# Decode attention with a gated MLP on one core: two heads per cache tile, and the values as the moving operand of the product with the probabilities

## The chip, the cores and the metric

The kernel runs on one core of one Trainium2 chip. The metric is device time in microseconds (us). The numbers below are medians. The profile is of one execution; its span is 1.7 to 1.9 us shorter than the time of the same execution. In the views, PE stands for the matmuls of TensorE, PEld for its weight loads, DVE for VectorE, ACT for ScalarE, POOL for GpSimd and SP for SyncE. A packet is one piece that a DMA engine moves at a time, for K and V one row of one partition (in the kernel before 16 KB, 613 ns in the median).

## The reference

This is one decode step: four sequences, one new token each, 32 heads with 8192 cached keys and values of 128 elements, then a gated MLP. Everything in memory is bf16.

```python
B, D = 4, 512;  H, Sk, Dh = 32, 8192, 128;  F = 1792

def attn(x, k_cache, v_cache, wq, wo):             # caches: B x H x Sk x Dh
    q = (x @ wq).reshape(B, 1, H, Dh).transpose(0, 2, 1, 3)
    scores = einsum("bhqd,bhkd->bhqk", q, k_cache) * Dh ** -0.5
    p = softmax(scores)
    o = einsum("bhqk,bhkd->bhqd", p, v_cache)
    return o.transpose(0, 2, 1, 3).reshape(B, 1, H * Dh) @ wo

def mlp(x, w_gate, w_up, w_down):
    return (sigmoid(x @ w_gate) * (x @ w_up)) @ w_down

h  = x + attn(layernorm(x), k_cache, v_cache, wq, wo)
h2 = h + mlp(layernorm(h), w_gate, w_up, w_down)
```

There are 128 pairs of sequence and head. Each has 2 MB of keys (K) and 2 MB of values (V), so the caches are 537 MB of the 550.8 MB that must be read. Each byte is used once.

## The kernel before

The kernel has its own small scheduler. Each operation `P(engine, function, deps)` is put on one engine's list in program order, and its dependencies become semaphore waits. The parts that the change touches are these.

Loads go through one queue, issued in order by SyncE, into a ring of 8 slots of 2 MB. One load fills a slot with one head: 128 partitions, each a row of 16 KB. A load waits until the operation that consumed its slot's last content has ended. The loads of the output weights (`wo`) go into the buffer `kT`, so they wait for the last score.

```python
NS = 8                                             # slots
items = [("wq", 0)]
for t in range(NT + LAG):                          # NT = 128 heads, LAG = 10
    if t < NT:    items.append(("k", t))
    if t >= LAG:  items.append(("v", t - LAG))
    if NT + 1 <= t <= NT + NWO:  items.append(("wo", t - NT - 1))   # 8 loads of 512 KB
items += [("wg", 0), ("wu", 0), ("wd", 0)]         # wd in two pieces

def kv_src(t, cache):
    return cache[t // H, t % H, :, :].rearrange("(p r) d -> p (r d)", p=128)
...
for it in items:
    for op in dma_of[it]:
        op.deps = [sc_of[NT - 1]] if it[0] == "wo" else [consumed[p] for p in prev_of[it]]
```

VectorE transposes each K tile into `kT` (line 366, four operations of 128x1024 uint32 per head, 1213 ns each). TensorE then computes scores with q as weights (line 383, 16 matmuls of 512 columns per head). Eight heads share one softmax chain. The product with V uses each 128x128 block of V as *weights* and one column of probabilities as the moving operand, 64 times per head:

```python
# pe_pv, line 406
for r in range(r0, r1):                            # 64 blocks of V
    c0 = (r % 16) * 32 + (r // 16) * 8 + hh
    mm = e.matmul(ob[:, hh:hh + 1], ringv(slot)[:, r * 128:(r + 1) * 128],
                  PT_sb[:, g % 2, c0:c0 + 1], start=(r == 0), stop=(r == R - 1))
```

At the end, the down projection has the hidden vector as weights and `w_down` moving; the residual had been put into the accumulator by four small matmuls beforehand.

```python
for i, (t0, t1) in enumerate(WD_PARTS):            # [(0, 10), (10, 14)]
    for s_ in range(2):
        ...                                        # line 602
        for t in range(t0, t1):
            mm = e.matmul(bP[s_][0:B, 0:HD], hh_sb[:, B * t:B * t + B],
                          wd_v[:, t, HD * s_:HD * s_ + HD], ...)     # 256 columns
```

## Time and profile before

| | before |
|---|---|
| time, median of the first 3 runs (lowest to highest) | 1318.3 us (1317.25 to 1318.69) |
| span of the profile | 1316.8 us |
| bytes from HBM | 550.77 MB |
| packets for K and V | 32,640 of 16 KB, median 613 ns; 256 of 8 KB |
| packets on the instruction queue | 92 |

The first view is the profile's page: the span, the busy times of the engines, the DMA totals, two of its queues (packets, MB, share of 16 engines), and three of its costliest groups (line, engine, operation, shapes, count, then busy us and mean ns of one, then idle time before it and what ended it).

```profile
span 1316.8 us, 24848 instructions
PE 527.4 (40%) x11822; PEld 330.1 (25%) x11822; DVE 628.7 (48%) x639; ACT 39.2 (3%) x87; POOL 9.7 (1%) x17
DMA packets 44757, 552.37 MB, mean 419 GB/s; under 512 B 4328, under 2 KB 10224, under 8 KB 11248
q1 hardware_dynamic: 44648, 550.79, 98.9%
q8 instruction: 92, 1.51, 0.5%
...
L366 DVE STREAM_TRANSPOSE kT<-ring 128x1024 uint32<-128x1024 uint32 x512 | 592.3, 1213 | 596.6 <-DMA ring<-in_A_k_cache_dram 596.6
L406 PEld LDWEIGHTS PS<-PT_sb,ring 128*128 128x128 bf16 x8192 | 230.1, 104 | 114.6 <-issue 76.6
L406 PE MATMUL PS<-PT_sb,ring 128*128 128x1 bf16 x8192 | 239.2, 165 | 38.0 <-DMA ring<-in_A_v_cache_dram 35.3
```

No engine is busy half of the time, while the queue of loads is busy 98.9% of it.

A table of stretches of the span: stretch and length, then for each engine its busy time and count, then the TensorE clock that the throttle granted (1.00 is full speed), the mean DMA share of 16 engines, and the rate.

```profile
core 0: us, PE busy (x) PEld busy (x) DVE busy (x) ACT busy (x) POOL busy (x), PEclk, DMA share, GB/s
400.00:1200.00 800.00, 318.06 (x7170) 197.92 (x7170) 383.52 (x384) 15.46 (x40) 0.00 (x0) 0.50 1.01 427
...
1218.00:1236.00 18.00, 5.98 (x113) 3.13 (x114) 9.58 (x9) 0.00 (x0) 0.00 (x0) 0.50 0.74 314
1236.00:1251.00 15.00, 7.86 (x282) 7.33 (x279) 1.33 (x6) 3.03 (x6) 0.00 (x0) 0.50 0.99 395
```

For 800 us the stream runs without a gap. Near the end, from 1218 to 1236 us, the mean share drops to 0.74. The waits of the queue itself (us in total, times, longest) give the reason: the first of the `wo` loads waits at the head of the queue for the last score.

```profile
SPq L207 <- PE PS L383: 27.6, 1, 27.6
```

The last view is the end of the chain of waits (start, length, what):

```profile
1286.08 22.63 DMA ring<-in_B_w_down_dram
1308.70 0.14 issue
1308.84 5.76 PE PS L602 x28
1314.60 0.02 issue
1314.62 0.41 DVE o_sb L607
```

### The profile page before, as it was taken

What the parts mean: (1) busy time and instruction counts of PE and PEld (TensorE: products, weight loads), DVE (VectorE), ACT (ScalarE), POOL (GpSimd) and SP (SyncE); (2) the same over time, 40 slices, a digit from 0 to 9 for tenths busy, and PEclk for the clock granted to TensorE, in tenths of its full rate; (3) what the DMA queues carried; (4) which work ended last, traced back from release to release, by engine and by line L of the source; (5) the groups of instructions that cost most, each with busy time, mean ns of one, the idle gap of its engine ahead of it and who ended that gap; (6) DMA issues with size and microseconds to landing.
All of it is one profiled execution on the core that took longest, in us unless ns stands there. A gap on an engine that the chain in (4) does not pass through costs nothing.

```text
span 1316.8 us, 24848 instructions
## 1 busy us (share of the span) xinstructions
PE 527.4 (40%) x11822; PEld 330.1 (25%) x11822; DVE 628.7 (48%) x639; ACT 39.2 (3%) x87; POOL 9.7 (1%) x17
## 2 busy tenths in 40 slices
PE   2453433433343343443343343343334334344435
PEld 1122222222232232222222222222222223222334
DVE  6965445445444544544545444544544544554300
ACT  3000000000000000000000000000000000000000
POOL 2000000000000000000000000000000000000000
PEclk8555555555555555555555555555555555555555
DMA  9999999999999999999999999999999999999896
GB/s 397 425 428 427 427 429 425 427 426 427 426 428 427 426 427 427 426 428 428 425 429 427 427 427 427 426 428 427 426 427 427 427 427 426 428 426 428 351 408 258
DMA packets 44757, 552.37 MB, mean 419 GB/s; under 512 B 4328, under 2 KB 10224, under 8 KB 11248
## 3 DMA queue, kind: packets, MB, share of 16 engines
q1 hardware_dynamic: 44648, 550.79, 98.9%
q8 instruction: 92, 1.51, 0.5%
q14 instruction: 9, 0.07, 0.0%
q10 hardware_dynamic: 8, 0.00, 0.0%
HBM read 550.77 MB, written 0.00 MB: 418 GB/s over the span
## 4 chain that ended last, share of the span: by engine, by line
DMA 85%; DVE 12%; issue 2%; PE 1%; SPq 0%
DMA ring<-in_A_k_cache_dram 77%; DVE kT L366 11%; DMA ring<-in_A_v_cache_dram 6%; DMA ring<-in_B_w_down_dram 2%; DMA ring<-in_A_wq_dram 1%; PE PS L602 0%; DVE Lq L349 0%; PE PS L406 0%; PE PS L307 0%; DVE ring L324 0%; PE PS L383 0%; PE PS L334 0%; SPq L241 0%; SPq L207 0%; DVE o_sb L607 0%
## 5 line engine op out<-in xcount | busy, mean ns | idle before, releaser
L366 DVE STREAM_TRANSPOSE kT<-ring 128x1024 uint32<-128x1024 uint32 x512 | 592.3, 1213 | 596.6 <-DMA ring<-in_A_k_cache_dram 596.6
L383 PE MATMUL PS<-kT,Lq 128*32 128x512 bf16 x2048 | 242.9, 623 | 664.3 <-DVE kT L366 664.3
L406 PEld LDWEIGHTS PS<-PT_sb,ring 128*128 128x128 bf16 x8192 | 230.1, 104 | 114.6 <-issue 76.6
L406 PE MATMUL PS<-PT_sb,ring 128*128 128x1 bf16 x8192 | 239.2, 165 | 38.0 <-DMA ring<-in_A_v_cache_dram 35.3
L383 PEld LDWEIGHTS PS<-kT,Lq 128*32 128x32 bf16 x2048 | 57.3, 126 | 751.4 <-DVE kT L366 680.5
L445 ACT ACTIVATE negm<-PS 128x1 f32<-128x1 f32 x16 | 2.7, 171 | 1166.9 <-PE PS L441 1166.9
L456 PE MATMUL PS<-LS,onesf 128*128 128x8 f32 x32 | 9.5, 372 | 64.9 <-DVE LS L452 64.9
L478 DVE TENSOR_TENSOR OT<-PS,rinv 128x8 bf16<-128x8 f32 (+2 forms) x17 | 2.0, 115 | 52.0 <-PE PS L406 52.0
L456 PEld LDWEIGHTS PS<-LS,onesf 128*128 128x128 f32 x32 | 8.0, 312 | 66.6 <-DVE LS L452 66.5
L467 PE MATMUL PS<-Sel,E_sb 128*32 128x32 bf16 x1024 | 11.4, 192 | 2.8 <-issue 1.7
L424 DVE TENSOR_REDUCE mx<-PS 128x1 f32<-128x512 f32 x16 | 10.5, 657 | 2.0 <-PE PS L383 2.0
L441 PEld LDWEIGHTS PS<-onesf,rowx 1*128 1x128 f32 x32 | 8.0, 307 | 12.6 <-issue 12.6
L447 ACT ACTIVATE E_sb<-PS,negm 128x512 bf16<-128x512 f32 x16 | 11.0, 687 | 0.5
L473 ACT ACTIVATE PT_sb<-PS 128x512 bf16<-128x512 f32 x16 | 9.6, 597 | 27.5 <-PE PS L467 27.5
L467 PEld LDWEIGHTS PS<-Sel,E_sb 128*32 128x32 bf16 x1024 | 9.5, 103 | 3.2 <-issue 1.8
L441 PE MATMUL PS<-onesf,rowx 1*128 1x1 f32 x32 | 9.3, 358 | 0.0
L259 POOL MEMSET Lq<- 128x8208 f32 x1 | 6.9, 6937 | 0.0
L349 DVE CAST Lq<-PS 32x128 bf16<-32x128 f32 x8 | 5.7, 712 | 2.1 <-PE PS L334 1.9
L602 PE MATMUL PS<-ring,hh_sb 128*4 128x256 bf16 x28 | 5.7, 397 | 1.8 <-DMA ring<-in_B_w_down_dram 1.8
L277 DVE TENSOR_SCALAR xpad<-x_bf,lnst 4x512 bf16<-4x512 bf16 x1 | 6.0, 5981 | 0.0
L430 PE MATMUL PS<-identf,mx 128*1 128x128 f32 x16 | 5.9, 371 | 0.0
L348 ACT ACTIVATE Lq<-PS 32x128 bf16<-32x128 f32 x8 | 5.7, 715 | 4.2 <-PE PS L334 4.0
(69 smaller groups left out, 71.3 us busy)
## 6 DMA issues: line engine op xcount, KB each, us to landing
ring<-in_A_k_cache_dram SPq DMA_DIRECT2D x128, 2048.0 KB, 34.6
ring<-in_A_v_cache_dram SPq DMA_DIRECT2D x127, 2048.0 KB, 35.8
ring<-in_A_wq_dram SPq DMA_DIRECT2D x1, 4096.0 KB, 12.5
kT<-in_A_wo_dram SPq DMA_DIRECT2D x8, 512.0 KB, 17.1
ring<-in_A_v_cache_dram SPq DMA_DIRECT2D x2, 1024.0 KB, 20.7
ring<-in_B_w_gate_dram SPq DMA_DIRECT2D x1, 1792.0 KB, 20.9
ring<-in_B_w_up_dram SPq DMA_DIRECT2D x1, 1792.0 KB, 25.3
ring<-in_B_w_down_dram SPq DMA_DIRECT2D x1, 1280.0 KB, 22.6
```

The lines of the kernel that those rows point to most:

```text
L259: zlq = pool(lambda e: e.memset(Lq[:, :].bitcast(FP32), 0.0))
L277: d_x = P("dve", lambda e: e.tensor_scalar(xpad[0:B, :], x_bf[0:B, :], st[0:B, 0:1], st[0:B, 4:5], op0=ALU.subtract, op1=ALU.mult), [d_r, zx])
L366: return e.transpose(kT[:, buf, i * q:(i + 1) * q].bitcast(U32), ringv(src)[:, i * q:(i + 1) * q].bitcast(U32))
L383: mm = e.matmul(bS[g % 2][32 * j:32 * (j + 1), :], Lq[:, l0:l0 + 32], rhs, start=(hh == 0 and v == 0), stop=(hh == GH - 1 and v == 3), til ...
L406: mm = e.matmul(ob[:, hh:hh + 1], ringv(slot)[:, r * 128:(r + 1) * 128], PT_sb[:, g % 2, c0:c0 + 1], start=(r == 0), stop=(r == R - 1))
L424: mx_of[g] = P("dve", lambda e: e.tensor_reduce(mx[:, :], bS[g % 2][:, :], AX.X, ALU.max), [sc_of[g * GH + GH - 1], p1_of.get(g - 1)])
L430: p1_of[g] = P("pe", lambda e: e.transpose(bX[0:1, 0:128], mx[:, :], identf[:, :]), [mx_of[g], c_identf, d3_of.get(g - 1)] + ([o for ops i ...
L441: p2_of[g] = P("pe", lambda e: e.matmul(bX[:, 0:1], rowx[0:1, :], onesf[0:1, 0:1], start=True, stop=True), [d2b_of[g], c_ones])
L447: exp_of[g] = P("act", lambda e: e.activation(E_sb[:, :], bS[g % 2][:, :], ACT.Exp, bias=negm[:, 0:1], scale=SCALE, accum_out=sig[:, 0:1]) ...
L456: L_of[g] = P("pe", lambda e: e.matmul(bX[:, 0:GH], onesf[:, :], LS[:, :], start=True, stop=True), [LS_of[g], a1_of[g], c_ones])
L467: mm = e.matmul(bP[g % 2][32 * a:32 * (a + 1), 32 * rr:32 * rr + 32], E_sb[:, 32 * rr:32 * rr + 32], Sel[:, a, :], start=True, stop=True, ...
L473: ptc_of[g] = P("act", lambda e: e.activation(PT_sb[:, g % 2, :], bP[g % 2][:, :], ACT.Copy), [pt_of[g]] + last_pv)
```

## The change

Its intent is to read the caches in rows twice as long, and to replace the weight loads of the product with V by long moving operands. It has these parts.

- A tile holds two heads, 64 partitions each, with rows of 32 KB. The ring has 4 slots of 4 MB: the same bytes.
- The weights of the product with V are now columns of probabilities, padded with zeros to 32 columns so that each head and half of a tile adds into its own rows of the accumulator. V moves, 512 columns at a time: 16 matmuls per step in place of 64.
- The accumulator then holds more than is wanted; for every 8 heads it is scaled by the reciprocal sums, the wanted diagonal is gathered by four fp32 matmuls with a selection matrix, and copied to `OT`.
- The `wo` loads are queued among the last V loads. The last V tile comes in three pieces.
- `w_down` comes in three pieces and becomes the weights. An addition of the residual, one transposing matmul and a copy follow.

The diff, cut to its core:

```diff
-NS = 8
+NS = 4
@@ order of loads
-            if NT + 1 <= t <= NT + NWO:
-                items.append(("wo", t - NT - 1))
+            for i in {LAG2 - 4: (0, 1), LAG2 - 3: (2, 3, 4), LAG2 - 2: (5, 6, 7)}.get(t - NT2, ()):
+                items.append(("wo", i))
@@ source of a K or V tile
-            return cache[t // H, t % H, :, :].rearrange("(p r) d -> p (r d)", p=128)
+            h = 2 * t
+            return cache[h // H, h % H:h % H + 2, :, :].rearrange("h (p r) d -> (h p) (r d)", p=64)
@@ product with V
-                for r in range(r0, r1):
-                    c0 = (r % 16) * 32 + (r // 16) * 8 + hh
-                    mm = e.matmul(ob[:, hh:hh + 1], ringv(slot)[:, r * 128:(r + 1) * 128],
-                                  PT_sb[:, g % 2, c0:c0 + 1], start=(r == 0), stop=(r == R - 1))
+                for j in range(j0, j1):
+                    for rq in range(4):
+                        r0 = (u * 4 + j) * 16 + 4 * rq
+                        l0 = PZ0 + (rq * 32 + 8 * j + 4 * u + i) * 32 - 8 * i
+                        mm = e.matmul(bO[g % 2][32 * rq:32 * (rq + 1), :], PTz[:, g % 2, l0:l0 + 32],
+                                      ringv(slot)[:, r0 * 128:(r0 + 4) * 128],
+                                      start=(s % GS == 0 and j == 0), stop=(s % GS == GS - 1 and j == 3),
+                                      tile_position=(0, 32 * rq))
@@ after each group of 8
+        def chain_z(g):
+            z_of[g] = P("dve", lambda e: e.tensor_scalar(Zs[:, :], bO[g % 2][:, :], rinv[:, g % 2:g % 2 + 1], None,
+                                                         op0=ALU.mult), ...)
+        def chain_ot(g):
+                for r in range(4):
+                    mm = e.matmul(bX[:, 256:264], Zs[:, 128 * r:128 * (r + 1)], SelZ[:, r, :], start=(r == 0), stop=(r == 3))
+        def chain_otc(g):
+            otc_of[g] = P("dve", lambda e: e.tensor_copy(OT[:, 8 * g:8 * g + 8], bX[:, 256:264]), [ot_of[g]])
@@ down projection
-                        mm = e.matmul(bP[s_][0:B, 0:HD], hh_sb[:, B * t:B * t + B], wd_v[:, t, HD * s_:HD * s_ + HD],
-                                      start=False, stop=(t == NFT - 1), skip_group_check=True)
+                    for c in range(NDC):
+                        mm = e.matmul(bH[:, B * c:B * c + B], wd_v[:, t, 128 * c:128 * (c + 1)],
+                                      hh_sb[:, B * t:B * t + B], ...)
+        d_o = P("dve", ... h2 + bH -> oT ...)
+        p_o = P("pe", lambda e: e.matmul(bP[0][0:NB, 0:128], oT[:, :], ident[:, :], start=True, stop=True), ...)
+        o0 = P("dve", lambda e: e.tensor_copy(o_sb[:, :], bP[0][0:NB, 0:128]), [p_o])
```

Cut: setting up the selection matrices, the re-indexing of scores and softmax for two heads, `wq` read in rows of 32 KB, the weights of gate and up in one slot, and the writing of the padded probabilities.

## The prediction

> **What bounds it now.** The HBM read stream. The table of stretches shows 427 GB/s and a DMA share of 1.01 in every stretch from 40 to 1200 us; the page has VectorE busy 48%, TensorE 40%. The chain of waits is 85% DMA; its transposes of K only mark slots coming free. Mid-run work on TensorE (PV busy 239 us) and VectorE is off the critical path. Three other costs:
>
> 1. A hole near the end. The output-weight loads wait in the SP queue for the last score (27.6 us in its own waits); from 1218 to 1236 us the share is 0.74 (314 GB/s). The DMA records sum the idle to 5.0 us.
> 2. The tail after the last w_down piece (landed 1308.8): 28 matmuls of 256 columns, 5.74 us, a 0.4 us copy, the store.
> 3. A fixed cost in each packet. Median packet times: 1 KB 46 ns, 3.5 KB 140, 8 KB 309, 16 KB 613: slope about 27.2 B/ns (16 engines: 435 GB/s), intercept about 8.4 ns.[...]
>
> **What the change does.**
> - K and V: 32768 packets of 16 KB become 16384 of 32 KB. Estimate from the fit: 1216 ns each against 2 x 613 = 1226; 8 packets per engine and load, 128 loads: about 0.08 x 128 = 8 to 10 us with the halved completion packets. I take 8.
> - The hole: output weights are queued after V loads that cover them; by the order of slots the last score ends about 16 us before the queue would run dry. Gain 5 us.
> - Ring of 4 slots instead of 8, same bytes. A K slot is held 8 transposes = 9.7 us (1213 ns each), a V slot about 6 us after landing; reloads are issued over 10 us before the queue drains. No cost.
> - PV: 64 weight loads of 128 columns with one-column matmuls (1.86 us a head) become 16 matmuls of 32x512, the form of the score matmuls (1.90 us). No change in time, fewer weight loads.
> - Per 8 heads: a 512-column scale (about 0.65 us, like the max), four fp32 selection matmuls (about 2 us), a copy. Hidden, except in the last group.
> - Tail: the last group's scale, selection and 32 output-weight matmuls add about 2.8 us to the chain from the last V byte, part of which was waiting for w_up before. Then w_down as weights: 56 matmuls at about 29 ns = 1.65 us instead of 5.74, plus 0.9 us of small steps. Net gain about 3.
>
> Sum: 16 us of 1318: **1302 us**, 80% range 1296 to 1311. Chances: faster by over 2% 0.03, within 2% 0.95, slower 0.02.
>
> **What would show it right or wrong.** 32 KB packets of about 1216 ns (if rows are cut at 16 KB, no gain: about 1310). Steady rate 430 to 431 GB/s. DMA share near 1.0 where the hole was. Last w_down landing to end of the last matmul under 3 us. Weight-load busy falling from 330 us to about 150.
>
> **What would make it wrong.** [...]four slots leave the queue short at the start or where groups end; the longer last chain ends well after w_down lands; three output-weight loads of 1 KB packets in a row starve the queue.

(Two passages are cut: one that only gave a reference, and a risk about the distance between the engines' reads, which no trace or run shows. No term of the sum is among them: 8 + 5 + 3 = 16 us. The sizes are estimates. The profile before has, for the estimate of the scale, the max at 657 ns; for the selection, fp32 matmuls of 8 columns at 372 ns and their weight loads at 312; and for `w_down` as weights, the 112 matmuls of gate and up in 3.3 us, 29 ns each.)

## More of the kernel before

The product with V is 8192 weight loads and 8192 matmuls: two thirds of all 24,848 instructions.

## The result, and the profile after

| | before | after |
|---|---|---|
| time in the same rounds, median of 4 (lowest to highest) | 1318.49 us (1317.25 to 1319.09) | 1296.41 us (1296.24 to 1296.48) |
| ratio, 95% interval | | 0.9834 (0.9816 to 0.9851) |
| span | 1316.8 us | 1294.5 us |
| packets for K and V (median) | 32,640 of 16 KB (613 ns), 256 of 8 KB | 16,256 of 32 KB (1216 ns), 128 of 16 KB, 256 of 8 KB |
| instructions | 24,848 | 12,693 |

Here and below, a ratio is the mean time of one kernel's runs over that of the other's of the same rounds, so it is not quite the ratio of the medians. The kernel before is timed again in each session; its session medians lie between 1317.65 and 1318.49 us, so a difference between two kernels of different sessions is uncertain by about 0.8 us (0.06%).

The change gains 22.1 us (22.3 in the span). The lines of the page after that answer to those before:

```profile
span 1294.5 us, 12693 instructions
PE 499.5 (39%) x5827; PEld 193.4 (15%) x5827; DVE 625.4 (48%) x641; ACT 46.1 (4%) x102; POOL 10.6 (1%) x22
DMA packets 26076, 551.58 MB, mean 426 GB/s; under 512 B 2340, under 2 KB 8232, under 8 KB 9256
q1 hardware_dynamic: 26016, 550.78, 99.5%
q8 instruction: 45, 0.74, 0.2%
...
L439 PE MATMUL PS<-ring,PTz 128*32 128x512 bf16 x2048 | 215.0, 564 | 208.7 <-DMA ring<-in_A_v_cache_dram 208.3
```

TensorE is hardly less busy than before (499.5 for 527.4 us) and VectorE as busy as before. What has halved is the count of instructions, and with it the line of q8: 45 packets for 92. The stretches after:

```profile
400.00:1200.00 800.00, 303.15 (x3387) 112.47 (x3390) 392.06 (x389) 21.34 (x50) 0.00 (x0) 0.60 1.00 431
...
1218.00:1236.00 18.00, 8.61 (x141) 3.72 (x133) 2.00 (x5) 3.62 (x7) 0.00 (x0) 0.69 1.00 414
1236.00:1251.00 15.00, 7.40 (x60) 3.81 (x64) 0.17 (x1) 0.00 (x0) 0.00 (x0) 0.50 0.93 353
```

The rate is 431 in place of 427 GB/s, and the drop to 0.74 between 1218 and 1236 us is gone; a lesser one, to 0.93, follows it. The queue still waits for the last score, but less long:

```profile
SPq L220 <- PE PS L415: 19.2, 1, 19.2
```

The end of the chain:

```profile
1279.05 12.10 DMA ring<-in_B_w_down_dram
1291.14 0.04 issue
1291.19 0.60 PE PS L637 x16
...
1292.37 0.28 DVE o_sb L648
```

From the landing of the last piece of `w_down` (1291.14) to the end of the last copy it takes 1.5 us.

### Where the landings of one load lie

One more reading decides most of what follows. Each load lands in 16 shares, and each share signals its landing by itself with a 4-byte packet: the kernel before has 4320 of them for its 270 loads, the kernel after 2304 for 144. So the DMA records give, for each load, 16 landing times. The core has 16 DMA engines, and I take each share for the part of one engine. The spread between the first and the last of the 16, computed from these records, grows steadily through the run (us, near the times given):

| time in the run | 13 | 200 | 400 | 600 | 800 | 1000 | 1200 | 1220 |
|---|---|---|---|---|---|---|---|---|
| before | 0.4 | 3.5 | 6.4 | 8.2 | 11.5 | 14.6 | 17.3 | 17.4 |
| after | 0.6 | 2.2 | 3.3 | 4.9 | 6.4 | 7.9 | 8.4 | 9.6 |

Within one load seven of the 16 landings come early, one lies between, and eight come late (us after the first of them; loads near 1219 and 1217 us):

```
before  0.0 0.3 0.4 0.5 0.7 1.1 2.1  6.2 | 15.7 15.7 15.9 15.9 16.1 16.2 17.3 17.4
after   0.0 0.2 0.2 0.2 0.4 0.8 0.9  5.1 |  7.7  7.8  7.9  8.0  8.1  8.3  8.4  9.6
```

Eight engines run behind the rest, in the kernel before twice as far as in the kernel after. A tile is there only when the last share is, since its users wait for all 16: where VectorE is free, the first transpose of a K tile starts 0.02 us after the last of its landings, in both kernels. So the late half sets the time, and a mean over 16 engines hides it.

### The profile page after: what moved, and what is told of

Its sections match the earlier page's. It is cut to its first block, busy times and chain, and to the rows that moved or that the text cites. A ratio compares the mean times of both kernels' runs of the same rounds, so it can differ in the third digit from the quotient of the medians.

```text
span 1294.5 us, 12693 instructions
## 1 busy us (share of the span) xinstructions
PE 499.5 (39%) x5827; PEld 193.4 (15%) x5827; DVE 625.4 (48%) x641; ACT 46.1 (4%) x102; POOL 10.6 (1%) x22
## 3 DMA queue, kind: packets, MB, share of 16 engines
q1 hardware_dynamic: 26016, 550.78, 99.5%
## 4 chain that ended last, share of the span: by engine, by line
DMA 81%; PE 12%; SPq 4%; DVE 3%; issue 0%
DMA ring<-in_A_v_cache_dram 79%; PE PS L439 7%; PE PS L415 4%; SPq L220 2%; DVE kT L397 2%; SPq L236 1%; DMA ring<-in_A_wq_dram 1%; DMA ring<-in_B_w_down_dram 1%; SPq L228 1%; SPq L256 0%; PE PS L330 0%; DVE Lq L374 0%; DVE ring L347 0%; PE PS L357 0%; PE PS L637 0%
## 5 line engine op out<-in xcount | busy, mean ns | idle before, releaser
L439 PE MATMUL PS<-ring,PTz 128*32 128x512 bf16 x2048 | 215.0, 564 | 208.7 <-DMA ring<-in_A_v_cache_dram 208.3
L415 PEld LDWEIGHTS PS<-kT,Lq 128*32 128x32 bf16 x2048 | 69.4, 135 | 692.4 <-DVE kT L397 471.9
L439 PEld LDWEIGHTS PS<-ring,PTz 128*32 128x32 bf16 x2048 | 64.5, 127 | 326.4 <-DMA ring<-in_A_v_cache_dram 197.1
L511 DVE TENSOR_SCALAR Zs<-PS,rinv 128x512 f32<-128x512 f32 x16 | 11.6, 723 | 36.4 <-PE PS L439 36.4
L506 ACT ACTIVATE PTz<-PS 64x512 bf16<-64x512 f32 x32 | 18.9, 592 | 16.5 <-PE PS L492 16.1
L518 PE MATMUL PS<-SelZ,Zs 128*128 128x8 f32 x128 | 19.1, 276 | 0.9 <-DVE Zs L511 0.9
L518 PEld LDWEIGHTS PS<-SelZ,Zs 128*128 128x128 f32 x128 | 17.6, 213 | 10.6 <-issue 8.9
L481 PEld LDWEIGHTS PS<-sig,Gsum 128*128 128x128 f32 x32 | 7.8, 305 | 12.6 <-issue 12.6
L481 PE MATMUL PS<-sig,Gsum 128*128 128x1 f32 x32 | 9.2, 356 | 0.0
## 6 DMA issues: line engine op xcount, KB each, us to landing
kT<-in_A_wo_dram SPq DMA_DIRECT2D x8, 512.0 KB, 17.3
```

The lines of the kernel that those rows point to most:

```text
L415: mm = e.matmul(bS[g % 2][32 * j:32 * (j + 1), :], Lq[:, l0:l0 + 32], rhs, start=(s % GS == 0 and v == 0), stop=(s % GS == GS - 1 and v == 3),
L439: mm = e.matmul(bO[g % 2][32 * rq:32 * (rq + 1), :], PTz[:, g % 2, l0:l0 + 32], ringv(slot)[:, r0 * 128:(r0 + 4) * 128], start=(s % GS == ...
L481: L_of[g] = P("pe", lambda e: e.matmul(bX[:, 0:1], Gsum[:, :], sig[:, 0:1], start=True, stop=True), [exp_of[g], a1_of[g], d_g])
L506: return e.activation(dst, src, ACT.Copy)
L511: z_of[g] = P("dve", lambda e: e.tensor_scalar(Zs[:, :], bO[g % 2][:, :], rinv[:, g % 2:g % 2 + 1], None, op0=ALU.mult), [pv_of[g * GS + G ...
L518: mm = e.matmul(bX[:, 256:264], Zs[:, 128 * r:128 * (r + 1)], SelZ[:, r, :], start=(r == 0), stop=(r == 3))
```

## The experiments

I began with the prediction's theory (T1: packets 8 us, hole 5 us, tail 3 us; instructions cost nothing). The rivals were that the rate rose for some other reason than the rows, that fewer instructions or less TensorE time mattered (T2), and, after the first results, that a part of the gain lay in how far the late engines run behind (T3).

| run | from | what was done | time, us (lowest to highest) | ratio to before (95%) | q8 packets |
|---|---|---|---|---|---|
| e1_split16 | after | rows of 16 KB | 1306.05 (1305.95 to 1306.15) | 0.9912 (0.9898 to 0.9925) | 45 |
| e1_split8 | after | rows of 8 KB | 1324.93 (1324.76 to 1324.99) | 1.0055 (1.0042 to 1.0067) | 45 |
| e2_instr | after | 48 tiny matmuls more per step | 1305.58 (1305.38 to 1305.71) | 0.9908 (0.9894 to 0.9921) | 93 |
| e3_petime | after | 4 long matmuls more per step | 1298.17 (1297.65 to 1298.29) | 0.9851 (0.9838 to 0.9864) | 49 |
| e4_wo_late | before | `wo` queued later | 1317.22 (1316.96 to 1318.52) | 0.9999 (0.9986 to 1.0011) | 92 |
| e5_down | before | new down projection | 1315.07 (1314.86 to 1315.13) | 0.998 (0.9967 to 0.9994) | 92 |
| e6_wo_down | before | both of these | 1314.91 (1314.63 to 1314.99) | 0.9979 (0.9966 to 0.9991) | 92 |
| e8_rows | after | longer rows of the small weights | 1300.26 (1299.84 to 1300.37) | 0.9867 (0.9854 to 0.9881) | 45 |
| e11_balance | after | one V load given to fewer partitions | 1326.91 (1324.48 to 1328.28) | 1.0069 (1.0056 to 1.0082) | 45 |
| e12_both | after | 16 KB rows and 48 tiny matmuls | 1314.96 (1314.51 to 1315.06) | 0.9978 (0.9965 to 0.9992) | 92 |
| e9_ns3 | after | 3 slots | 1298.5 (1298.29 to 1298.88) | 0.9855 (0.9841 to 0.9868) | 45 |
| e14_few | after | a quarter of the matmuls | 1292.05 (1291.85 to 1292.13) | 0.9802 (0.9788 to 0.9815) | 21 |

### Is it the length of the rows?

Each K or V load of the changed kernel is cut into two (or four) loads of half (a quarter of) the row. Nothing else changes.

```diff
+            if kind in ("k", "v"):
+                uses[slot] += 2                       # 4 in e1_split8
+                ...                                   # sem, val, src
+                W = TW // 2                           # TW // 4
+                return [(lambda e, c0=i * W: e.dma_start(ringv(slot)[:, c0:c0 + W],
+                                                         src[:, c0:c0 + W]).then_inc(sem, 16), sem, val)
+                        for i in range(2)]            # range(4)
```

> The changed kernel with every K and V load cut into two loads of 16 KB rows; engines, slots and tail untouched. Packet theory: each 32 KB packet (median 1216 ns) becomes two of 613 ns, 10 ns x 8 packets x 128 loads = 10.5 us, and twice the completion packets (2048 x 9 ns / 16 engines = 1.1 us): about 1308 us, steady rate 427 to 428 GB/s instead of 431. Rival (the gain in rate comes from the other engines or from fewer instructions to fetch): no change, about 1297 us.

> The same with four loads of 8 KB rows for each K and V load. Packet theory: four packets of 309 ns for one of 1216, 20 ns x 8 x 128 = 20.5 us, and four times the completion packets, 3.4 us: about 1320 us, steady rate about 423 GB/s. Rival: about 1297 us.

The stretch of each from 400 to 1200 us, e1_split16 first:

```profile
400.00:1200.00 800.00, 305.21 (x3370) 113.64 (x3362) 387.45 (x385) 21.32 (x50) 0.00 (x0) 0.59 1.01 428
400.00:1200.00 800.00, 300.93 (x3334) 112.26 (x3330) 383.04 (x381) 21.32 (x50) 0.00 (x0) 0.60 1.01 421
```

With rows of 16 KB the time was 1306.05 us, 9.6 more than the changed kernel, and the rate from 400 to 1200 us was 428 for 431 GB/s. With rows of 8 KB it was 1324.93, 28.5 more, at 421 GB/s: slower than the kernel before, with all the rest of the change in place. The median times of one packet are 309 ns for 8 KB, 613 for 16 KB and 1216 for 32 KB. They lie on the straight line that the prediction used: 2 x 613 - 1216 = 10 ns, a fixed cost in each packet. The fixed cost is 8 to 10 ns a packet and is worth 0.7% of the run at 16 KB; what it consists of, no run shows. So the rows gain 9.6 us, where 8 was predicted. With 8 KB the cost was above the 1320 us expected. In that run a packet of 8 KB took 313 ns (the 309 are from the kernel before), and the 4-byte completion packets (9 ns each in the changed kernel) grew from 2325 to 8421; I did not separate the two.

### Was the hole lost time?

In the kernel before, `wo` is queued two to four V loads later, so that the queue holds more work while it waits for the last score.

```diff
-            if NT + 1 <= t <= NT + NWO:
-                items.append(("wo", t - NT - 1))
+            for i in {3: (0,), 4: (1, 2), 5: (3,), 6: (4, 5), 7: (6,), 8: (7,)}.get(t - NT, ()):
+                items.append(("wo", i))
```

> The kernel before, with its eight output-weight loads queued two to four V loads later, so that the wait for the last score stands behind V loads; nothing else. If the hole was 5.0 us of idle queue that nothing gives back: about 1313 us, ratio 0.996 to 0.997; if, as in the changed kernel's trace, some 1.3 us of idle stays[...]: about 1314. If the tail swallows it: 1318.

The time was 1317.22 us against 1317.65 for the kernel before in the session: ratio 0.9999, nothing gained. The stretches of e4_wo_late show what happened to the hole:

```profile
1218.00:1236.00 18.00, 6.43 (x130) 3.59 (x131) 9.94 (x9) 0.00 (x0) 0.00 (x0) 0.50 1.00 422
1236.00:1251.00 15.00, 8.44 (x297) 7.83 (x294) 0.96 (x5) 3.03 (x6) 0.00 (x0) 0.50 0.80 326
```

From 1218 to 1236 us the share is now 1.00, and from 1236 to 1251 it is 0.80. The hole moved and shrank: 0.26 of 18 us is 4.7 us of mean idle time, 0.20 of 15 us is 3.0. The wait for the last score is shorter than before (17.4 us for 27.6). Yet the time is unchanged, where 1313 to 1314 us had been expected.

The spread of landings explains why. In the hole of the kernel before, the spread falls from 17.7 to 6.4 us: the early engines have run dry and wait while the late ones work on. About seven of 16 engines idle for 11.3 us, and 11.3 x 7 / 16 = 4.9 us, which is the 5.0 us of mean idle time that the prediction summed. The late engines, which decide when a tile is complete, were not idle in it: through the hole the last landings of successive loads of 2 MB stay 4.8 to 5.3 us apart, as before it, with 1.4 us more where a `wo` load lies between. The prediction took idle time averaged over engines for time lost.

### What is the tail worth?

The kernel before gets the changed kernel's down projection alone (e5_down), and together with the late `wo` (e6_wo_down).

```diff
-        (four matmuls that put the residual into bP; w_down as moving operand; two half copies)
+        p_d.append(P("pe", pe_down, [d_hh, dma_of[("wd", 0)][i], d_h]))      # w_down as weights, still two pieces
+        d_o = P("dve", ... oT = h2 + bH ...)
+        p_o = P("pe", lambda e: e.matmul(bP[0][0:NB, 0:128], oT[:, :], ident[:, :], start=True, stop=True), ...)
+        o0 = P("dve", lambda e: e.tensor_copy(o_sb[:, :], bP[0][0:NB, 0:128]), [p_o])
```

> The kernel before, with the down projection alone as in the changed kernel (w_down as weights, 4 columns of hidden values moving, residual added on VectorE, one transposing matmul, one copy, 16-row store); w_down still in two pieces. Last landing to the end of the span was 8.0 us before and 3.3 after: about 1313.5 us, ratio 0.9965. Rival (the longer chain of the last group matters as much as the down projection, and the form alone is worth less): 1316 or more.

> The kernel before with both of these edits: the sum, about 1309.5 us, ratio 0.993 to 0.994. What then separates it from the changed kernel (1296.4), about 13 us, is the steady rate alone: packets of 32 KB (10 us) and fewer instruction fetches (about 4 us, from the 16 KB-row run's steady 427.0 GB/s of K and V against 425.6 before).

The new tail gains 2.6 us by the medians (1315.07 for 1317.65), where about 4 had been expected. In the profiled spans it is 3.7 us (1313.1 for 1316.8), but the profiled execution of the kernel before was one of its slower ones: 1318.69 us, 1.0 above its median. The end of the chain of e5_down:

```profile
1308.55 1.20 PE PS L592 x40
1309.76 0.04 issue
1309.79 0.60 PE PS L592 x16
```

The first piece of `w_down` lands at about 1308.5 us and its 40 matmuls end at 1309.76; the last piece lands at 1309.7 by the DMA records, and the last 16 take 0.60 us. In the changed kernel the last piece lands at 1291.14 us, 18.6 earlier. Of the 22.3 us between the spans, 3.7 are thus the tail, and the stream ends 18.6 us sooner. (The medians give 18.7 from e5_down to the changed kernel.) Adding the late `wo` gives 1314.91, no more than the tail alone: the second measurement in which the hole is worth nothing.

### Then what else moved the end of the stream by 18.6 us? Instructions or TensorE time

The rows account for 9.6 of it, and the hole for none. The two runs below were made to show that fewer instructions and less TensorE time do not matter. In e2_instr, 48 one-column matmuls are added to every step of the product with V but the last two, which brings the count of instructions back to that of the kernel before. In e3_petime, four matmuls of 512 columns are added to the same steps: much TensorE time, few instructions. The results of the extra matmuls are never read.

```diff
@@ e2_instr, in pe_pv after the loop
+                if piece is None:
+                    for _ in range(48):
+                        mm = e.matmul(bH[:, 300:301], ident[:, :], ident[:, 0:1], start=True, stop=True)
@@ e3_petime, in the same place
+                if piece is None:
+                    for q in range(4):
+                        mm = e.matmul(bH[:, :], ident[:, :], ringv(slot)[:, 512 * q:512 * q + 512],
+                                      start=True, stop=True)
```

> The changed kernel with 48 one-column matmuls (128 weights each) added after each PV step but the last two, results unused: about 6000 more matmuls with their weight loads, so about as many instructions as the kernel before (24,848). Instruction-fetch theory: fetch packets rise from 45 to about 92 of 16 KB, 0.77 MB more through the same 16 engines, at 427 GB/s 1.8 us, at most 3.1 us if each holds an engine for its measured 1.05 us: 1298 to 1300 us. Theory that TensorE time matters (about 1.4 us more per step): a larger loss, 1305 us or more. Rival (fetch costs nothing): 1296.4.

> The changed kernel with 4 matmuls of 128x512 added after each PV step but the last two, results unused: about 1.7 us more TensorE work per step at the clock granted before (some 215 us in all, doubling PV), but only about 1000 more instructions (504 matmuls with weight loads). If TensorE in mid-run is off the critical path: 1296 to 1297 us. If TensorE time sets when V slots come free and that matters: 1305 us or more.

e2_instr was a clear miss of my expectation: 1305.58 us, 9.2 above the changed kernel, where I had expected 2 to 3 for the fetching of instructions, and had put 1305 us or more down to TensorE time. e3_petime was at 1298.17, 1.8 above; in its profile TensorE waits 1.91 in place of 0.64 us for the last piece of `w_down`. The pages of the two:

```profile
span 1303.6 us, 24789 instructions
PE 707.2 (54%) x11875; PEld 355.4 (27%) x11875; DVE 625.2 (48%) x641; ACT 46.0 (4%) x102; POOL 10.6 (1%) x22
...
q8 instruction: 93, 1.52, 0.5%
```

```profile
span 1295.8 us, 13638 instructions
PE 609.6 (47%) x6268; PEld 216.3 (17%) x6331; DVE 625.6 (48%) x641; ACT 46.0 (4%) x102; POOL 10.6 (1%) x22
...
q8 instruction: 49, 0.80, 0.3%
```

110 us more of TensorE time (at least: 63 of the added matmuls have no record) cost 1.8 us, and 0.8 of that answers to four more packets of q8 at the rate found below. If time on TensorE were the cause, the 208 us more of e2_instr should have cost 3.4, not 9.2. What differs in e2_instr is the line of q8. Its packets hold 16 KB each (1.52 MB in 93). The 23,750 matmuls and weight loads of e2_instr make 255 to a packet, the 11,654 of the changed kernel 259: this is TensorE's part of the program, fetched by DMA while it runs (in the changed kernel the 45 packets start between 21.9 and 1288.8 us). The 48 packets more cost 9.2 us, 0.19 us each, in a kernel whose DMA engines have nothing to spare (the queue of loads is busy 99.5% of the span of the changed kernel).

The spread of landings shows where they act. In e2_instr, with the same loads as the changed kernel but the program size of the kernel before, it grows as in the kernel before:

| time in the run | 200 | 400 | 600 | 800 | 1000 | 1200 | q8 packets |
|---|---|---|---|---|---|---|---|
| before | 3.5 | 6.4 | 8.2 | 11.5 | 14.6 | 17.3 | 92 |
| e2_instr | 3.5 | 6.5 | 8.2 | 11.3 | 14.3 | 17.2 | 93 |
| e3_petime | 2.1 | 3.7 | 5.0 | 6.5 | 8.0 | 9.5 | 49 |
| after | 2.2 | 3.3 | 4.9 | 6.4 | 7.9 | 8.4 | 45 |
| e14_few (next run) | 2.0 | 2.4 | 3.6 | 4.0 | 4.1 | 5.2 | 21 |

The spread follows the number of fetched blocks, whether the rows have 16 or 32 KB. This is T3: the fetches hold back one half of the DMA engines. The records name no engine, but the landings show which half it is: the early seven stay within 2.1 us of each other up to 1225 us, while the lag of the late eight behind them, summed over the eight, grows by 1.46 to 1.51 us with each fetched block, in all five kernels of the table.

### The same with fewer instructions

If T3 holds, a program smaller than that of the changed kernel must be faster still. In e14_few three quarters of the score matmuls and of those with V are left out, so its result is wrong. All loads are kept.

```diff
-                for v in range(4):                    # pe_score (cut: the stop flags)
+                for v in range(1):
-                for j in range(j0, j1):               # pe_pv
+                for j in range(j0, j0 + 1):
```

> The changed kernel with three quarters of the score matmuls and of the PV matmuls left out (wrong results on purpose; the same loads, transposes and waits): about 6100 fewer instructions with their weight loads, about 6500 in all. Slow-engine theory (each fetch of instructions holds back one of the 8 late DMA engines; 12,100 more instructions cost 9.2 us): 6100 fewer give back 4.6 us, about 1291.8 us, with some 21 fetch packets and a landing spread of 4 to 6 us late in the run instead of 8 to 9.6. Rival (fetches below the changed kernel's 45 are hidden, or the extra matmuls cost time by TensorE work): 1296 us.

```profile
span 1290.3 us, 6557 instructions
PE 218.4 (17%) x2759; PEld 97.6 (8%) x2759; DVE 625.6 (48%) x641; ACT 46.1 (4%) x102; POOL 10.6 (1%) x22
...
q8 instruction: 21, 0.34, 0.1%
```

It took 1292.05 us: 4.4 less than the changed kernel for 24 packets less, 0.18 each. By itself this run could also be read as less TensorE time; together with e3_petime and the spread, which is down to 5.2 us, it is not. From 21 to 93 packets the time rises by 13.5 us and the spread by 12 us, 0.19 and 0.17 per packet; the changed kernel, in between, lies 0.15 us from that line. The record of one fetched block is 1.07 us long. If each falls on one of the eight late engines, it delays them by 1.07 / 8 = 0.13 us on average, less than 0.19. The DMA records hold the rest: behind every fetched block from 100 to 1200 us (37 in the changed kernel, 79 in e2_instr) one 32 KB packet took 1.7 us in place of 1.216, about 0.5 us more. Together that is near the 1.5 us by which the summed lag grows, and 1.5 / 8 = 0.19. Why the packet behind a block takes longer stays open.

The comparison with the reference says little of the attention part in any of these kernels: presumably its contribution to the output is too small.

### Do the two causes add up?

e12_both has the rows of e1_split16 and the extra matmuls of e2_instr, in the changed kernel. If rows and fetches are all, it should be as slow as the kernel before with the new tail, e5_down.

```diff
+ the edit of e1_split16 and the edit of e2_instr
```

> The changed kernel with both 16 KB rows (9.7 us when alone) and the 48 extra small matmuls per PV step (9.2 us when alone). If packet size and instruction fetches are the whole of what the layout gave, the sum: about 1315 us, which is what the kernel before ran with only the new down projection (1315.1). If they overlap: 1309 to 1312.

It took 1314.96 us, 18.55 above the changed kernel, where 9.6 + 9.2 = 18.8; and e5_down took 1315.07. The steady rate is 427 GB/s, as in the kernel before. The extra fetches cost 8.9 us at 16 KB rows (1314.96 - 1306.05) and 9.2 at 32 KB. So the books close: rows and fetched instructions explain the 18.6 us of the stream, and the tail the rest. That the product with V runs over different operands, that the diagonal is gathered, and that there are two heads to a tile have no cost or gain of their own that these runs can see.

### Does the ring of four slots cost something?

```diff
-NS = 4
+NS = 3
```

> The changed kernel with 3 slots of 4 MB instead of 4. By the order of slots each reload is still issued more than 10 us before the late engines run dry: 1296 to 1298 us. If the depth of the queue matters (the early engines run up to 8 us ahead of the late ones): 1300 or more, with DMA share under 0.98 in mid-run.

1298.5 us, 2.1 above, with a DMA share of 1.00 from 400 to 1200 us. Even three slots keep the stream full in mid-run. By the DMA records the loss arises at the start: the last share of the third load lands at 35.6 us in place of 33.6, and the loads stay 1.5 to 2.1 us behind up to 1207 us. There is a second lesson in this run: between 790 and 1080 us the early engines lose another 2.4 us and the late ones nothing, so that the spread at 1200 us is 6.6 in place of 8.4 us with the same 45 blocks. Idle time of the early engines cost nothing here either. Four slots were enough, as predicted.

### Two attempts at a better version

The small weights are read in rows of 1 KB to 3.5 KB. In e8_rows those of the MLP are read in longer rows (14 KB for gate and up, 4 to 5 KB for down), by giving each partition neighbouring rows of the matrix; the matmuls then take their weight columns with a stride.

```diff
-                dst, src = wg_v, B_w_gate.rearrange("(c p) f -> p c f", p=128)
+                dst, src = wg_v, B_w_gate.rearrange("(p c) f -> p c f", p=128)     # w_up likewise
-                                           B_w_down.rearrange("(t p) f -> p t f", p=128)[:, t0:t1, :]
+                                           B_w_down.rearrange("(p t) f -> p t f", p=128)[:, t0:t1, :]
-                    mm = e.matmul(bk[:, B * t:B * t + B], wv[:, c, 128 * t:128 * (t + 1)],
+                    mm = e.matmul(bk[:, B * t:B * t + B], wv[:, c, t:F:NFT],          # stride 14
```

(`wo` and `w_down` as weights get a stride of 4 in the same way, and the last transposition becomes four matmuls.)

> The changed kernel with longer rows for the three feed-forward weights: w_gate and w_up in 14 KB rows instead of 3.5 KB, w_down in 4 to 5 KB rows instead of 1 KB, by strided columns of the weights on the TensorE side and a strided transposing write at the end. Packet theory: 1408 + 768 fewer packets x 8.4 ns / 16 = 1.1 us: about 1295.2 us. Rival (the chain from the last V byte, not the landing of w_down, now ends last, or strided weight loads are slower): 1296.4 or more.

It was slower, 1300.26 us. `w_down` now landed before it was wanted (in the changed kernel its matmuls waited 1.3 us for it, here for no load), but the 112 matmuls of gate and up took twice as long. The group from 1240 to 1300 us in e8_rows, and then the same group in the changed kernel:

```profile
L623 PE MATMUL PS<-hnT,ring 128*128 128x4 bf16 x112 | 6.9, 199 | 1.3 <-DVE hnT L614 1.3
```

```profile
L623 PE MATMUL PS<-hnT,ring 128*128 128x4 bf16 x112 | 3.2, 166 | 1.3 <-DVE hnT L614 1.3
```

The last four transposing matmuls and the copy took 1.03 + 0.68 us in place of 0.29 + 0.28. What the load gained, the strided weights on the path behind it gave back and more. A weight load took 161 ns in place of 104 with the stride of 14, and 117 to 118 in place of 103 to 105 with that of 4. Why a stride makes it longer was not tested.

e11_balance was to make the late engines catch up near the end, by giving one of the last V loads in nine parts: eight loads of 8 partitions for the lower half, and one of 64 for the upper.

```diff
+            if kind == "v" and t in (59,):               # cut: sem, val, src
+                cuts = [(8 * i, 8 * i + 8) for i in range(8)] + [(64, 128)]
+                uses[slot] += len(cuts)
+                return [(lambda e, a=a, b=b: e.dma_start(ringv(slot)[a:b, :], src[a:b, :]).then_inc(sem, 16),
+                         sem, val) for a, b in cuts]
```

> The changed kernel, with half of one late V load (partitions 0 to 63 of the last but four) issued as 8 loads of 8 partitions[...]. The landings of one load spread over 8.4 us late in the run, about 8 engines early and 8 late. Slow-engine theory (the 8 late engines set the end, the others wait for them)[...]. Rival (only the mean load of the 16 engines counts): 1296.4, unchanged.

(Depending on which engines are the late ones, I had expected about 1292 or about 1301 us. The trace has 64 more packets of 4 bytes than that of the changed kernel, which fits eight for each small load, but names no engine.)

It was 30 us slower, and says nothing about T3. The parts ran at half the rate with the engines counted as full:

```profile
1209.00:1239.00 30.00, 7.41 (x65) 2.27 (x65) 7.08 (x9) 0.00 (x0) 0.00 (x0) 0.56 1.02 200
```

A 32 KB packet took 2.5 us (median) here in place of 1.216. Why, no run shows. It was not this load alone: between 1206 and 1255 us 275 packets, 9.0 MB, took over 1.8 us each, and this load has 4 MB, so that loads around it were slowed too. Evening out the engines without such a loss stays untried. No run here beats the changed kernel with a correct result.

## Why the prediction was right or wrong

- **Right: the bound.** The stream from HBM bounds the kernel before and after: its queue is busy for 98.9 and 99.5% of the span. Work on TensorE in the middle is off the critical path: 110 us more of it cost at most 1.8.
- **Right: the rows.** Packets of 1216 ns came as estimated, the steady rate came to 431 GB/s, and the rows measured 9.6 us by e1_split16 for 8 predicted.
- **Right: the ring of four slots.** No cost was seen; three slots cost 2.1 us, at the start.
- **About right: the tail.** "Net gain about 3": 2.6 us timed. (The 3.7 in the span include the slower execution.) A detail was wrong: 1308.8 us was the landing of the first piece of `w_down`, not of the last, which came about a microsecond later.
- **Wrong: the hole.** "The DMA records sum the idle to 5.0 us", and "Gain 5 us". The sum was right, and it was not lost time: the early half of the engines waited in it for the late half. Queuing `wo` later, which moved it and made it smaller, gained 0.4 us in e4_wo_late, with an interval around zero, and 0.2 on top of the new tail in e6_wo_down.
- **Wrong, by a missing term: the instructions.** "No change in time, fewer weight loads." TensorE's time did not matter indeed, but the halved program did: 47 fetched blocks fewer on engines that were full. Put back (48), they cost 9.2 us in e2_instr and 8.9 in e12_both.
- **Small sizes.** Weight-load busy was 193.4 us for "about 150", the scale 723 ns for "about 0.65 us". Both are off the path.

| term | predicted, us | measured, us | by |
|---|---|---|---|
| rows of 32 KB | 8 | 9.6 | e1_split16 |
| hole | 5 | 0.4, not clear of 0 | e4_wo_late |
| fetched instructions | 0 | 9.2 | e2_instr, e12_both, e14_few |
| tail | 3 | 2.6 to 3.7 | e5_down |
| sum | 16 | 21.4 to 22.5, without the hole | timed: 22.1; 21.2 against the kernel before in the session of e5_down |

The time of 1296.41 us is 0.4 us above the lower end of the range. That the range held it was partly luck: one term counted 5 us that were not there, and another left out 9.

Shown: the worth of the rows, of the instructions and of the tail, each changed alone; that the first two add; that the lag of the late eight engines grows with the number of fetched blocks, by 1.5 us a block in sum; and that this comes to 0.19 us of time a block. Open: why the blocks fall on these eight, since the records name no engine; why the packet behind a block takes 0.5 us longer; and whether the engines could be evened out.

## What to carry to other kernels

In a kernel that keeps the DMA engines full, count every packet, also those of the program itself: here each fetched block of 16 KB, 255 to 259 instructions of TensorE, cost 0.19 us, though TensorE was busy for little over half of the time at most (54% in e2_instr). (The fetches of the other engines were not varied.) Before calling a dip in the mean DMA share lost time, look at the landings of the single shares of a load: here the late engines set the time, and the dip, 5.0 us of mean idle time, was the others waiting for them. And when a term of a sum is to be believed, undo it alone: the hole looked as solid as the rows in the profile and was worth nothing.
